# First x tile in halves by two queues, GpSimd in program order, one ScalarE copy ahead of two activations, the z sums in two parts

## The chip, the cores and the metric

One core of one Trainium2 chip. The metric is the device time of one execution in microseconds (us). The spans in the profiles are about 2 us shorter than the times of the same runs. The granted TensorE clock was 0.998 to 1.0. A ratio of two kernels is the mean time of one kernel's fast runs over that of the other's of the same rounds, so it is not quite the ratio of the medians that are quoted.

TensorE is PE, VectorE DVE, ScalarE ACT, GpSimd POOL, SyncE SP; "SPq" and "ACTq" are DMA issues. Tiles whose names begin with ps lie in PSUM, where TensorE writes its results; "to evacuate" is to copy them out. xr is a tile of x that is read back, hn a normalised h1, pk and pqa are phi of k and of q, wgu the gate and up weights.

## The reference, cut to what matters

A transformer block, forward and all gradients (`jax.vjp`), for S = 2048 rows of D = 640 in bf16, that is 16 tiles of 128 rows:

```
q, k, v = split(layernorm(x) @ wqkv)             # 32 heads of 20
phi(t)  = where(t > 0, t + 1, exp(t)) + 1e-6
pq, pk  = phi(q), phi(k)
kv      = einsum("bhsd,bhse->bhde", pk, v);  z = pk.sum over s
o       = (pq @ kv) / (pq . z + 1e-6)
h       = x + o @ wo
out     = h + (silu(layernorm(h) @ w_gate) * (layernorm(h) @ w_up)) @ w_down
# returned: out and the gradients of x and of the weights
```

## The kernel before

The first place is the k/q loop (0 to 58 us): per tile, VectorE takes the row statistics, GpSimd makes the reciprocal root, VectorE normalises, TensorE transposes, ScalarE copies the transpose out of PSUM, TensorE multiplies by the k and q weights, ScalarE makes exp and relu, VectorE joins them to pk and pqa.

```python
load_x(nc.sync, 0, 1)                       # x tile 0
load_x(nc.scalar, 1, 2)                     # x tile 1
nc.sync.dma_start(out=wqk[:, 0:3, D:2 * D], in_=w_k[:, 0:3, :])    # k weights, 480 KB
nc.sync.dma_start(out=wqk[:, 3:5, D:2 * D], in_=w_k[:, 3:5, :])    # 320 KB
# ... x tile 2, q weights, ... issued once the statistics of tile 0 are done

def ln_rstd(mv, rstd, t0, nt, eng=nc.gpsimd):
    v = small.tile([P, 4], FP32, name="lnv", tag="lnv")
    eng.tensor_scalar(out=v[:, :nt], in0=mv[:, :nt, 1], scalar1=1e-5, scalar2=None, op0=ALU.add)
    nc.gpsimd.tensor_tensor(out=rstd[:, t0:t0 + nt], in0=v[:, :nt], in1=nhalf[:, :nt], op=ALU.pow)

with tc.manual_schedule(engines={EngineType.PE, EngineType.DVE, EngineType.Activation}):
    # ... cut: tile 0, warm-up matmuls, statistics of tiles 1 and 2
    kq_mm(1, 0)()                           # k of tile 1, then its exp and relu
    kq_mm(0, 1)()                           # q of tile 0, then its exp and relu
    for t in range(1, ST):
        if t == 1:
            ln1(2)                          # normalise, transpose, copy tile 2
        if t > 1:
            kq_mm(t, 0, (lambda: ln1(t + 1)) if t + 1 < ST else None)()
        # ... cut: kq_phi (VectorE), statistics of tile t + 2
        kq_mm(t, 1)()
    ps = mm("ps_z")                         # sums of pk over all rows
    for ci, (n0, n1) in enumerate(NCH):     # two column halves
        for t in range(ST):
            nc.tensor.matmul(ps[q:q + H, ci, :320], lhsT=ones[:, :H], rhs=pk[:, t, n0:n1], ...)
```

The order of the engines named in `manual_schedule` is that of the program; GpSimd isn't among them, so the scheduler places its instructions. After z comes ps_y; its first matmul is the milestone that I use for "end of the first stage".

The second place is the stage from about 108 to 149 us, in which x is read back for the residual, tile by tile, while the first group of gate and up weights is loaded:

```python
def load_xr(t):
    if t < ST:
        xrs[t] = wk("xr")                   # one of 5 work buffers
        nc.sync.dma_start(out=xrs[t][:], in_=x_v[:, t, :])

for t in range(ST + 2):
    if t < ST:
        # ... cut: ps_a = attention output of tile t
        nc.vector.tensor_tensor(out=half(xr[:]), in0=row(ps), in1=half(xr[:]), op=ALU.add)   # h1
        # ... cut: its statistics
        dm(1)                               # ps_dm matmuls, ScalarE evacuates them to dmst
    if t > 0:
        load_xr(t + 2)
    # ... cut
    nc.scalar.dma_start(out=scr_h1_v[:, u, :], in_=h1[:])            # store of h1, u = t - 2
    # ... cut: hn, and its transpose by DMA

def load_wgu(g):
    nc.sync.dma_start(out=t[:, :, 0:w], in_=B_w_gate[...])           # 560 KB
    nc.sync.dma_start(out=t[:, :, w:2 * w], in_=B_w_up[...])         # 560 KB
```

Of the kernel before, what the change touches and what calls it, by code (L numbers as in the profile page):

```python
# [13 lines left out]
EngineType = mybir.EngineType  # L14
# [6 lines left out]
def kernel(  # L21
# [8 lines left out]
    nc = tc.nc  # L30
# [3 lines left out]
    ST = S // P  # L34
    DT = D // P
    NCH = [(0, 320), (320, 640)]
# [12 lines left out]
    x_v = A_x.rearrange("b (t p) d -> p (b t) d", p=P)  # L49
# [13 lines left out]
    def mm(name):  # L63

        return psum.tile([P, 2, 512], FP32, name=name, tag="mm")

    def row(ps):
        return ps[:, :, :320]

    def half(ap):  # L70
        return ap.rearrange("p (c n) -> p c n", c=2)
# [3 lines left out]
    def wk(name, w=D, pool=0):  # L75
        return wpools[pool].tile([P, w], BF16, name=name, tag="w", padded_shape=[P, D])
# [99 lines left out]
    def fw(name):  # L176
        return wpool.tile([P, 2, GM], BF16, name=name, tag="f", bufs=6)
# [9 lines left out]
    x_tm = [strips.tile([P, 8, D], BF16, name="x_tm", tag="S") for _ in range(2)]  # L187
# [6 lines left out]
    def load_x(eng, t0, t1):  # L194
        return eng.dma_start(out=x_tm[t0 // 8][:, t0 % 8:(t1 - 1) % 8 + 1, :], in_=x_v[:, t0:t1, :])

    load_x(nc.sync, 0, 1)
    load_x(nc.scalar, 1, 2)
    w_k = A_wqkv[:, D:2 * D].rearrange("(k p) n -> p k n", p=P)
    w_q = A_wqkv[:, 0:D].rearrange("(k p) n -> p k n", p=P)  # L200
# [3 lines left out]
    def wait_for(on, dmas):  # L204
        info = mybir.DependencyInfo(mybir.DependencyClass.Sync, mybir.DependencyReason.DATA)
        for dma in dmas:
            tc.add_manual_dep(dma.ins, on.ins.name, info, reason="paced")
# [7 lines left out]
    def load_3():  # L215
        for t0 in range(4, ST, 2):
            yield load_x(nc.sync, t0, t0 + 2)
        yield nc.sync.dma_start(out=wvo[:, 0:5], in_=A_wqkv[:, 2 * D:3 * D].rearrange("(k p) n -> p k n", p=P))
        for j in range(HG):
            yield nc.sync.dma_start(out=wvo[:, 5 + j, :], in_=A_wo[OH[j]:OH[j] + P, :])  # L220
        yield load_wdT(wdT, 0)
        for c in range(4):
            yield nc.sync.dma_start_transpose(out=dh2T[:, :, c * 512:(c + 1) * 512], in_=go_flat[c * 512:(c + 1) * 512, :])
        yield load_wdT(wdT, 1)
        yield load_wdT(wdT3, 3)
# [38 lines left out]
    def ln1_stats(t):  # L264
        st = ln_stats(x_tm[t // 8][:, t % 8, :], mv1[:, t, :])
        if t == 0:
            wait_for(st, load_2())

    def ln1_xn(t):
        nc.vector.tensor_scalar(out=xn[:, t, :], in0=x_tm[t // 8][:, t % 8, :], scalar1=mv1[:, t, 0:1],  # L270
                                scalar2=rstd1[:, t:t + 1], op0=ALU.subtract, op1=ALU.mult)

    def ln1_rstd(t):
        ln_rstd(mv1[:, t:t + 1, :], rstd1, t, 1)

    def ln1(t):
        if t < NC:
            nc.vector.tensor_scalar(out=xn[:, t, :], in0=x_tm[t // 8][:, t % 8, :], scalar1=mv1[:, t, 0:1],
                                    scalar2=None, op0=ALU.subtract)
        else:  # L280
            ln1_xn(t)
        tp = psum.tile([P, D], BF16, name="ps_t", tag="mm")
        for kt in range(DT):
            nc.tensor.transpose(tp[:, kt * P:(kt + 1) * P], xn[:, t, kt * P:(kt + 1) * P], ident[:])
        tpv = tp[:].rearrange("p (k c) -> p k c", c=P)
        if t == 0:
            wait_for(nc.scalar.copy(out=xnT[:, t, 0:3], in_=tpv[:, 0:3]), load_3())
            nc.scalar.copy(out=xnT[:, t, 3:5], in_=tpv[:, 3:5])
        else:
            nc.scalar.copy(out=xnT[:, t], in_=tpv)  # L290

    def kq_mm(t, which, between=None):
        dst, w0 = ((pk, D), (pqa, 0))[which]
        ps = mm("ps_kq")
        for k0, k1 in ((0, 3), (3, DT)) if t == 0 else ((0, DT),):
            for ci, (n0, n1) in enumerate(NCH):
                for k in range(k0, k1):
                    nc.tensor.matmul(ps[:, ci, :320], lhsT=xnT[:, t, k, :], rhs=wqk[:, k, w0 + n0:w0 + n1],  # L298
                                     start=(k == 0), stop=(k == DT - 1))
            if between and (t > 0 or k0 == 0):  # L300
                between()

        def act():
            e = fw("phi_e")
            r = fw("phi_r")
            sc = rstd1[:, t:t + 1] if t < NC else 1.0
            nc.scalar.activation(out=e[:, :, :320], in_=row(ps), func=ACT.Exp, scale=sc)
            nc.scalar.activation(out=r[:, :, :320], in_=row(ps), func=ACT.Relu, scale=sc)  # L308
            ers.setdefault(t, []).append((dst, e, r))

        return act

    def kq_phi(t, last=True):
        n = len(ers[t]) if last else 1
        for _ in range(n):
            dst, e, r = ers[t].pop(0)
            nc.vector.tensor_scalar(out=e[:, :, :320], in0=e[:, :, :320], scalar1=1.0, scalar2=1e-6,
                                    op0=ALU.min, op1=ALU.add)
            nc.vector.tensor_tensor(out=half(dst[:, t, :]), in0=e[:, :, :320], in1=r[:, :, :320], op=ALU.add)
        if last and t % 4 == 3:  # L320
            sl = slice(t - 3, t + 1)
            nc.sync.dma_start(out=scr_pk_v[:, sl, :], in_=pk[:, sl, :])
            nc.sync.dma_start(out=scr_pq_v[:, sl, :], in_=pqa[:, sl, :])
            nc.sync.dma_start(out=scr_xnT[sl].rearrange("t p k c -> p t k c"), in_=xnT[:, sl])

    with tc.manual_schedule(engines={EngineType.PE, EngineType.DVE, EngineType.Activation}):

        ps = mm("ps_warm")

        def warm(n):  # L330
            for _ in range(n):
                nc.tensor.matmul(ps[:, 0, :P], lhsT=ident[:], rhs=ident[:], start=True, stop=True)

        warm(31)
        ln1_stats(0)
        ln1_rstd(0)
        ln1(0)
        warm(12)
        ln1_stats(1)
        ln1_rstd(1)  # L340
        kq_mm(0, 0, lambda: ln1(1))()
        ln1_stats(2)
        ln1_rstd(2)
        kq_mm(1, 0)()
        kq_mm(0, 1)()
        for t in range(1, ST):
            if t == 1:
                ln1(2)
            if t > 1:
                kq_mm(t, 0, (lambda: ln1(t + 1)) if t + 1 < ST else None)()  # L350
            if t == 2:
                kq_phi(0)
            if t + 2 < ST:
                ln1_stats(t + 2)
                ln1_rstd(t + 2)
            if t == 1:
                kq_phi(0, last=False)
            kq_mm(t, 1)()
            if t > 1:
                kq_phi(t - 1)  # L360
            if t >= ST - NC:
                ln1_xn(t - ST + NC)
        kq_phi(ST - 1)


        ps = mm("ps_z")
        for ci, (n0, n1) in enumerate(NCH):
            for t in range(ST):
                q = t % 4 * H
                nc.tensor.matmul(ps[q:q + H, ci, :320], lhsT=ones[:, :H], rhs=pk[:, t, n0:n1],  # L370
                                 start=(t < 4), stop=(t >= ST - 4))
        zs = [wk("zs"), wk("zl")]
        nc.scalar.copy(out=half(zs[0][:]), in_=row(ps))
        last_zs = nc.vector.tensor_tensor(out=half(zs[1][:]), in0=row(ps), in1=half(zs[0][:]), op=ALU.subtract).ins
        ps_z = mm("ps_zb")
# [599 lines left out]
```

## Time and profile before

| | kernel before |
|---|---|
| time, 3 runs | 822.63 us (822.4 to 823.15) |
| span of the profiled run | 820.8 us |
| TensorE busy | 814.0 us, 99% |
| first statistics / third copy / first ps_y | 3.96 / 13.46 / 57.68 us |

How to read it: TensorE is busy nearly all the time, so only its idle time can be won. The lines that carry this stand in the prediction.

### The profile page before, as it was taken

Reading aid. Unit: us, or ns where it says so; the run is one execution under the profiler, and the core shown is the slowest. Engines: PE = TensorE matmul, PEld = TensorE weight load, DVE = VectorE, ACT = ScalarE, POOL = GpSimd, SP = SyncE. Lnnn points to the kernel's source line nnn. Section 1 sums busy time; section 2 is a strip of 40 time slices with the busy share of each in tenths; the row PEclk is TensorE's granted clock in tenths of the full one; section 3 lists DMA queues with packets and bytes.
Section 4 is the critical chain, followed back from the end, with each engine's and each line's share of the span. In section 5 each row is a group of like instructions: output and inputs, shape, how many; then the busy total and the mean of one; then the engine's idle time right before and its main releaser. Section 6 shows DMA issues by size and latency. Waiting matters only on the chain.

```text
span 820.8 us, 14051 instructions
## 1 busy us (share of the span) xinstructions
PE 814.0 (99%) x5540; PEld 523.4 (64%) x5540; DVE 443.8 (54%) x875; ACT 291.5 (36%) x412; POOL 187.4 (23%) x345
## 2 busy tenths in 40 slices
PE   8999999999999999999999999999999999999998
PEld 6776656555555555555566677777776777777776
DVE  6888686891087018800760157887884366631222
ACT  6982422770184126400841122323312133322101
POOL 2330022322412412221125301211210121112330
PEclk9999999999999999999999999999999999999999
DMA  9994589998769997894498757985497989899952
GB/s 295 194 351 95 141 183 276 306 203 176 191 127 209 199 220 168 185 246 111 107 244 180 246 141 213 217 209 161 124 235 172 165 162 176 170 185 258 257 155 73
DMA packets 278241, 158.53 MB, mean 193 GB/s; under 512 B 235036, under 2 KB 264797, under 8 KB 278176
## 3 DMA queue, kind: packets, MB, share of 16 engines
q1 hardware_dynamic: 251616, 82.04, 52.7%
q0 software_dynamic: 17744, 64.45, 24.9%
q10 hardware_dynamic: 8816, 11.16, 4.3%
q8 instruction: 43, 0.70, 0.3%
q14 instruction: 22, 0.18, 0.1%
HBM read 47.60 MB, written 53.66 MB: 123 GB/s over the span
## 4 chain that ended last, share of the span: by engine, by line
PE 87%; DVE 6%; ACT 3%; DMA 2%; issue 1%; SPq 1%; POOL 0%; DVEq 0%; ACTq 0%
PE ps_dw L627 21%; PE ps_dhn L109 14%; PE ps_dxn L877 8%; PE ps_o L932 7%; PE pu L563 7%; PE pg L558 7%; PE ps_dwqk L109 5%; PE ps_y L109 3%; PE ps_dp L109 3%; PE ps_dk L109 3%; PE ps_gt L678 3%; PE pdm L385 2%; PE ps_dm L385 2%; DVE st L134 1%; ACT phi_r L308 1%; DMA xr<-in_A_x_dram 1%
## 5 line engine op out<-in xcount | busy, mean ns | idle before, releaser
L109 PE MATMUL ps_dhn<-wgT,cols 128*128 128x320 bf16 x864 | 119.5, 299 | 0.0
L627 PE MATMUL ps_dw<-dd,hn 128*128 128x448 bf16 (+1 forms) x640 | 118.8, 346 | 0.0
L109 PEld LDWEIGHTS <-cols 128*128 128x128 bf16 x864 | 84.5, 98 | 32.9
L627 PEld LDWEIGHTS <-hn 128*128 128x128 bf16 x640 | 62.6, 98 | 54.2
L629 DVE CAST dwev<-ps_dw 128x896 bf16<-128x896 f32 (+3 forms) x12 | 10.9, 907 | 123.2 <-PE ps_dw L627 123.2
L629 ACT CAST dwev<-ps_dw 128x896 bf16<-128x896 f32 (+1 forms) x20 | 17.6, 878 | 157.9 <-PE ps_dw L627 157.9
L592 POOL DMA_DIRECT2D scr_dT<-stg x64 | 34.6, 541 | 168.9 <-DMA stg<-dd 168.0
L147 DVE CUSTOM_DVE_ANT_0 lb_a<-lb_dy,hn 128x640 bf16<-128x640 bf16 x32 | 26.4, 825 | 75.4 <-ACT lb_dy L145 75.4
L563 PE MATMUL pu<-wgu,hnT 128*128 128x448 bf16 (+1 forms) x320 | 63.6, 346 | 0.0
L558 PE MATMUL pg<-wgu,hnT 128*128 128x448 bf16 (+1 forms) x320 | 63.6, 346 | 0.0
L932 PE MATMUL ps_o<-wd,mT 128*128 128x320 bf16 (+2 forms) x462 | 62.8, 295 | 0.0
L627 PE MATMUL ps_dw<-m_s,dh 128*128 128x448 bf16 (+1 forms) x320 | 60.4, 346 | 0.0
L877 PEld LDWEIGHTS <-ring 128*128 128x128 bf16 x480 | 47.0, 98 | 18.2
L932 PEld LDWEIGHTS <-mT 128*128 128x128 bf16 x462 | 44.0, 98 | 16.2 <-issue 0.3
L877 PE MATMUL ps_dxn<-wqkvT,ring 128*128 128x320 bf16 x320 | 51.3, 299 | 0.0
L627 PEld LDWEIGHTS <-dh 128*128 128x128 bf16 x320 | 31.3, 98 | 27.1
L563 PEld LDWEIGHTS <-hnT 128*128 128x128 bf16 x320 | 31.3, 98 | 27.1
L558 PEld LDWEIGHTS <-hnT 128*128 128x128 bf16 x320 | 31.3, 98 | 27.0
L385 PEld LDWEIGHTS <-dh2T 128*128 128x128 bf16 x320 | 31.1, 98 | 25.5 <-issue 0.6
L298 PE MATMUL ps_kq<-wqk,xnT 128*128 128x320 bf16 x320 | 46.4, 299 | 1.0 <-ACT xnT L290 1.0
L385 PE MATMUL ps_dm<-wdT,dh2T 128*128 128x448 bf16 (+1 forms) x240 | 46.9, 344 | 0.3 <-ACT dmst L399 0.2
L145 ACT ACTIVATE lb_dy<-ps_dhn,rstd 128x640 bf16<-128x640 f32 x16 | 12.7, 793 | 87.8 <-PE ps_dhn L109 87.8
(163 smaller groups left out, 1277.5 us busy)
## 6 DMA issues: line engine op xcount, KB each, us to landing
scr_dT<-stg POOLq DMA_DIRECT2D x48, 224.0 KB, 3.2
cols<-scr_dT POOLq DMA_DIRECT2D x6, 1728.0 KB, 8.5
scr_m<-m_s POOLq DMA_DIRECT2D x12, 448.0 KB, 4.5
cols<-scr_dT ACTq DMA_DIRECT2D x2, 1728.0 KB, 9.7
out_dram<-dwev POOLq DMA_DIRECT2D x30, 112.0 KB, 3.0
scr_dT<-stg POOLq DMA_DIRECT2D x16, 192.0 KB, 2.6
scr_pk<-pk SPq DMA_DIRECT2D x4, 640.0 KB, 7.8
scr_pq<-pqa SPq DMA_DIRECT2D x4, 640.0 KB, 8.1
```

The lines of the kernel that those rows point to most:

```text
L109: nc.tensor.matmul(ps[:, ci, :320], lhsT=lhs(k), rhs=rhs(k, *NCH[ci]), start=(start and k == 0), stop=(stop and k == n - 1))
L147: nc.vector.tensor_tensor_reduce(out=a[:], in0=dy[:], in1=xhat, scale=1.0, scalar=0.0, op0=ALU.mult, op1=ALU.add, accum_out=sums[:, 1:2])
L298: nc.tensor.matmul(ps[:, ci, :320], lhsT=xnT[:, t, k, :], rhs=wqk[:, k, w0 + n0:w0 + n1], start=(k == 0), stop=(k == DT - 1))
L385: nc.tensor.matmul(ps[:, c, :w], lhsT=dh2T[:, kt, (t + c) * P:(t + c + 1) * P], rhs=wdT[:, kt, o:o + w], start=(kt == 0), stop=(kt == DT - 1))
L558: nc.tensor.matmul(pg[:, c, :w], lhsT=hnT[:, kt, (t + c) * P:(t + c + 1) * P], rhs=wg[:, kt, 0:w], start=(kt == 0), stop=(kt == DT - 1))
L563: nc.tensor.matmul(pu[:, c, :w], lhsT=hnT[:, kt, (t + c) * P:(t + c + 1) * P], rhs=wg[:, kt, w:2 * w], start=(kt == 0), stop=(kt == DT - 1))
L592: nc.gpsimd.dma_start(out=scr_dT[t + c, :, KO[g]:KO[g] + GK[g], :], in_=stg[:, :GK[g], :])
L627: nc.tensor.matmul(ps[:, c, :w], lhsT=lhs(t), rhs=rhs(t), start=(t == 0), stop=(t == ST - 1))
L629: copy(out=ev[:, :len(parts), :w], in_=ps[:, :len(parts), :w])
L678: nc.tensor.matmul(ps[:, ci, :320], lhsT=dh1[:, t, i * P:(i + 1) * P], rhs=pqs_tm[:, t, n0:n1], start=(t == 0), stop=(t == ST - 1))
L877: nc.tensor.matmul(ps[:, ci, :320], lhsT=lhs[:, i, :], rhs=rhs[:, i, n0:n1], start=(k == 0 and i == 0), stop=(k == 2 and i == DT - 1))
L932: nc.tensor.matmul(po, lhsT=mT[:, t % 4, j, :], rhs=wd[:, j, n0:n1], start=(j == 0), stop=(j == FT - 1))
```

## The change

Its intent: begin sooner (the first tile in halves by two queues, the second behind it), give the first root sooner (GpSimd in program order), and close TensorE's hole at 14 us (the third transpose is copied before the exp and relu of q of tile 0). It also does the z sums in two parts, tiles 0 to 11 first, which its description doesn't mention.

```diff
-    load_x(nc.sync, 0, 1)
+    nc.sync.dma_start(out=x_tm[0][:, 0, 0:320], in_=x_v[:, 0, 0:320])
+    nc.scalar.dma_start(out=x_tm[0][:, 0, 320:640], in_=x_v[:, 0, 320:640])
     load_x(nc.scalar, 1, 2)
@@
-    with tc.manual_schedule(engines={EngineType.PE, EngineType.DVE, EngineType.Activation}):
+    with tc.manual_schedule(engines={EngineType.PE, EngineType.DVE, EngineType.Activation, EngineType.Pool}):
@@
-        kq_mm(0, 1)()
+        act = kq_mm(0, 1)
+        ln1(2)
+        act()
         for t in range(1, ST):
-            if t == 1:
-                ln1(2)
@@
-        for ci, (n0, n1) in enumerate(NCH):
-            for t in range(ST):
+        for ci, (n0, n1), t0, t1 in [(c, NCH[c], *r) for r in ((0, 12), (12, ST)) for c in range(2)]:
+            for t in range(t0, t1):
```

## The prediction

> **What bounds the kernel now.** I read the page's busy line first, then TensorE's waits, then the timeline of the first 20 us and of 55 to 58 us, because the diff touches nothing later.
>
> ```profile
> PE 814.0 (99%) x5540; PEld 523.4 (64%) x5540; DVE 443.8 (54%) x875; ACT 291.5 (36%) x412; POOL 187.4 (23%) x345
> ```
>
> TensorE is busy for 814.0 of 820.8 us, and the change removes no matmul. All it can win is idle time: 6.8 us, part of it the unavoidable beginning and end. The view of TensorE's waits (us in total, times, longest) says where that idle time is:
>
> ```profile
> PE ps_warm L332 <- POOL ident masks.py:199: 1.4, 1, 1.4
> PE ps_kq L298 <- ACT xnT L290: 1.0, 2, 0.8
> PE ps_t L284 <- DVE xn L278: 0.7, 1, 0.7
> PE ps_dm L385 <- ACT dmst L399: 0.2, 1, 0.2
> ...
> PE ps_z L370 <- DVE pk L319: 0.2, 1, 0.2
> ```
>
> The change aims at the second, third and last of these, 1.9 us or 0.23% of the time. So the answer is "within 2%" before any detail, and the work is to find the tenths. The timeline of the start (start, duration, what, idle before it):
>
> ```profile
> 0.79 0.40 ACTq L195 DMA_DIRECT2D x_tm<-in_A_x_dram  x1
> ...
> 0.80 0.40 SPq L195 DMA_DIRECT2D x_tm<-in_A_x_dram  x1
> ...
> 3.96 0.89 DVE L134 BATCH_NORM_STATS2 st<-x_tm 128x6 f32<-128x320 bf16 x2 [2.59 <-DMA x_tm<-in_A_x_dram]
> ...
> 8.78 1.62 POOL L140 TENSOR_TENSOR rstd<-lnv,nhalf 128x1 f32<-128x1 f32 x3
> ...
> 9.39 0.79 ACT L307 ACTIVATE phi_e<-ps_kq,rstd 128x640 bf16<-128x640 f32 x1 [0.50 <-POOL rstd L140]
> ...
> 10.44 0.45 DVE L270 TENSOR_SCALAR xn<-x_tm,mv,rstd 128x640 bf16<-128x640 bf16 x1 [1.90 <-POOL rstd L140]
> ...
> 13.46 0.73 ACT L290 COPY xnT<-ps_t 128x640 bf16<-128x640 bf16 x1
> ...
> 14.25 1.53 PE L298 MATMUL ps_kq<-wqk,xnT 128*128 128x320 bf16 x10 [0.77 <-ACT xnT L290]
> ```
>
> Three things are to be seen. Nothing starts before the first x tile lands (3.96 us). GpSimd makes the first reciprocal root only at 8.78 us, after the "lnv" of all three first tiles, which holds ScalarE for 0.50 and VectorE for 1.90 us. ScalarE copies the third transpose at 13.46 us, behind six phi passes, though it was ready at about 12.1 us; TensorE stands for it.
>
> **What the Trainium skill says.** "DMA: Bandwidth & Descriptors", section "Issuing engines are not separate DMA queues": transfers from any engine run on the same 16 DMA engines and interleave; a second issuer saves only issue time. The trace agrees: the two 160 KB x tiles, issued together, took 3.14 and 3.0 us to land, the third, issued at 5.12 us nearly alone, 2.26 us. Its section "Queues, rings and completion order" adds that each DMA engine goes round its queues by packets. So the halves win nothing by using two queues as such; they win because the second tile no longer shares the engines with the first. "SBUF — State Buffer", section "SBUF: two separate sides": VectorE and GpSimd hold a shared port pair exclusively. The trace fits: the root takes 0.54 us (1.62 / 3) while VectorE is idle, 0.82 us beside its work later.
>
> **The change, part by part.** Against before, only three engine streams move: the first load is split, with ScalarE issuing one more DMA; GpSimd's order becomes lnv, root, lnv, root, lnv, root; and ScalarE's third copy moves ahead of phi(q) of tile 0. The order of VectorE is the same, and TensorE's differs only in the z sums.
>
> *Split load.* The first bytes move at 1.8 us; by 2.8 us 194 KB have moved, by 3.2 us 338 KB. The tile alone is 160 KB; with the other one 320 KB. If the two halves are served first, their bytes are in some 0.4 us earlier; rows of 640 instead of 1,280 bytes may take part of that back. Estimate: 0.35 us, range 0 to 0.6. The chain from there (statistics 0.89, aggregate 0.21, xn 0.39, transposes, copy 0.48, first k matmuls) is bound link by link until the matmuls at 8.95 us, so TensorE gets it in full, and the paced loads behind it move with it. The weights don't hold it: the DMA engines were empty from about 5.5 to 6.0 us. The second x tile lands later, but VectorE takes it only at 5.43 us, 1.6 us after it landed.
>
> *GpSimd's order.* The first root moves from 9.3 us to before 6.5, so phi of tile 0 starts 0.6 us earlier (about 8.8, after the copy). The third root comes at about 9.4 instead of 10.4, so xn of tile 2 is 1 us earlier. TensorE gains nothing by itself: it is in the matmuls from 8.95 to 11.7 us.
>
> *Third copy first.* Its transposes end at 11.68 + 0.44 = 12.12 us, so the copy runs 12.14 to 12.83 instead of 13.46 to 14.19. The ten matmuls of 11.96 us issue every 0.136 us until 13.32, so the next ten start there instead of 14.25. The hole is worth 0.93 us.
>
> *What the loop takes back.* phi(q) of tile 0 moves from 12.11 to 12.74, its second pass from 12.79 to 13.41, ending at 14.2. VectorE, in fixed order, waits for it: pqa of tile 0 starts at about 14.25 instead of 13.96, and VectorE has no slack after that (9.2 of 10 us busy). So pk of tile 1 ends at 16.5 instead of 16.2. The phi buffers hold three pairs, so ScalarE's first phi of tile 2 must wait for it: 16.6, where it could have been 16.0. That delays the PSUM slot for the transposes of tile 4 (17.98 instead of 17.67), the copy behind it, and the matmuls of tile 4: 19.73, where a closed hole would give 19.4 and before had 20.25. I worked the four engines forward in this way through all 16 tiles with the trace's spacings (matmul 0.136, transposes 0.27, phi 0.593, copy 0.60, VectorE 3.01 per tile). The same working gives before's z stage an end at 57.56 us, where the trace has 57.68, so I trust it to 0.1 us. About 0.42 us of 0.93 is left at the end of the loop.
>
> *z in two parts.* The lines:
>
> ```profile
> 56.01 0.72 PE L370 MATMUL ps_z<-pk,ones 128*32 128x320 bf16 x15
> 56.91 0.84 PE L370 MATMUL ps_z<-pk,ones 128*32 128x320 bf16 x17 [0.17 <-DVE pk L319]
> 57.68 4.52 PE L109 MATMUL ps_y<-pk,xn 128*128 128x320 bf16 x32
> ```
>
> Half of the z sums need the last pk after 15 matmuls, and the other 17 come behind it. In the new order 27 of 32 need no tile after 14. TensorE arrives 0.42 us earlier, while the last pk is earlier by only 0.26 us; 27 matmuls at 0.043 us cover that wait, and 5 follow instead of 17. The end of z moves from 57.56 to 56.80 in my working: 0.76 us with the 0.42 of the loop. With ScalarE spacings 0.02 us longer it is 0.5. I take 0.65.
>
> Sum: 0.35 + 0.65 = 1.0 us, 822.63 - 1.0 = 821.6 us.
>
> **Rivals.** *The hole closes and stays closed:* 0.93 for the hole, 0.3 for z and 0.35 for the load give 1.6 us, 821.0. For it: TensorE sets the period of the loop (2.997 us a tile), no wait shows after 14.25 us. Against: ScalarE and VectorE run at 3.0 us a tile too, so nothing can lead the others for long. *The loop takes everything back,* the copies return to 19.09, 22.09 and so on, and only load and z remain: about 822.1. For it: in my working ScalarE's fourth copy is at 18.98, no gain at all; it regains 0.3 afterwards because its spacings have 0.03 us of slack. *The split does nothing,* since the fixed latency dominates or the short rows cost what the order wins: 822.0. *A later stage swallows the gain:* the only later wait of TensorE in the first 140 us is 0.2 us at 137 us, on an evacuation whose chain runs through reloads of x (5.59 us for one). That chain starts at a matmul at 87.97 us, so it should move along. If it doesn't: 822.5.
>
> **Range and chances.** The parts are uncertain by about 0.3 us each, and another build's DMA timing and run-to-run spread (822.4 to 823.15) add 0.4. 8 times in 10: 820.8 to 822.5. Faster or slower by 2% would be 16 us; nothing here is that large. Faster 0.005, within 2% 0.99, slower 0.005.
>
> **What would show it.** The first statistics start at about 3.6 us (split right), or at 3.9 (wrong). GpSimd alternates lnv and root, and the first phi starts 0.5 us sooner relative to the first statistics. The 0.77 wait on xnT disappears, but a wait of 0.1 to 0.4 us on xnT, xn or a phi appears by tile 4. The first ps_y matmul comes near 56.7 instead of 57.68 us. All later stages shift by the same amount; if ps_y is early and the end is not, a DMA wait between 90 and 140 us took it. My prediction is wrong if the loop closes fully, or if the first tile lands later than now.

## More of the kernel before

The batches ran on different chips, where the median of the kernel before was 822.59 to 823.5 us, so the order of two variants of different batches that lie a few tenths apart is not shown.

One more of VectorE's timeline is needed later; the columns are start, duration, instruction, operands:

```profile
13.96 0.49 DVE L319 TENSOR_TENSOR pqa<-phi_e,phi_r 128x640 bf16<-128x640 bf16 x1
14.37 0.88 DVE L134 BATCH_NORM_STATS2 st<-x_tm 128x6 f32<-128x320 bf16 x2
```

This is the first pqa, without a wait, and VectorE goes on at once: from here on it runs the loop at 3.015 us a tile. Its one large gap, 0.52 us at 25 us, is in all traces (0.51 to 0.53).

## The result, and the profile after

823.02 us median of 4 runs (822.04 to 823.76), the kernel before 822.59 with one more run beside it. The ratio is 1.0003, 95% interval 0.9986 to 1.0021: no difference, and 1.4 us above the prediction.

TensorE's waits in the profile after (us in total, times, longest):

```profile
PE ps_dm L386 <- ACT dmst L400: 0.8, 1, 0.8
PE ps_dxn L878 <- DMA ring<-dq: 0.5, 1, 0.5
PE ps_t L285 <- DVE xn L271: 0.3, 1, 0.3
PE ps_kq L299 <- ACT xnT L291: 0.2, 1, 0.2
...
PE ps_z L371 <- DVE pk L320: 0.2, 1, 0.2
```

The waits that the change aims at went from 1.9 us to 0.7. (The 0.3 for xn is a new one: it stands in the loop, at 26.5 us.) But the wait for dmst grew from 0.2 to 0.8, and one for a transposed dq came. The start in the timeline (line numbers are one up from before):

```profile
3.02 0.89 DVE L134 BATCH_NORM_STATS2 st<-x_tm 128x6 f32<-128x320 bf16 x2 [1.65 <-DMA x_tm<-in_A_x_dram]
...
5.39 0.89 DVE L134 BATCH_NORM_STATS2 st<-x_tm 128x6 f32<-128x320 bf16 x2 [0.82 <-DMA x_tm<-in_A_x_dram]
...
9.42 0.45 DVE L271 TENSOR_SCALAR xn<-x_tm,mv,rstd 128x640 bf16<-128x640 bf16 x1 [1.00 <-POOL rstd L140]
...
13.55 0.49 DVE L320 TENSOR_TENSOR pqa<-phi_e,phi_r 128x640 bf16<-128x640 bf16 x1 [0.36 <-ACT phi_r L309]
```

The first tile is there 0.94 us earlier, not 0.35. The second, which VectorE took without a wait at 5.43, now makes it wait 0.82 us, so a part of that is lost again: the copy of the second transpose starts at 7.49 us, before at 8.20. The third xn comes at 9.42 as predicted. The copy is where it should be and the hole is closed:

```profile
8.10 0.79 ACT L308 ACTIVATE phi_e<-ps_kq,rstd 128x640 bf16<-128x640 f32 x1
...
11.44 0.69 ACT L291 COPY xnT<-ps_t 128x640 bf16<-128x640 bf16 x1
```

And the end of the stage:

```profile
55.11 1.13 PE L371 MATMUL ps_z<-pk,ones 128*32 128x320 bf16 x27
56.41 0.43 PE L371 MATMUL ps_z<-pk,ones 128*32 128x320 bf16 x5 [0.17 <-DVE pk L320]
56.77 4.52 PE L109 MATMUL ps_y<-pk,xn 128*128 128x320 bf16 x32
```

ps_y starts at 56.77 us; before it was 57.68, and 56.7 was predicted. So 0.91 us were won here. The lead is 0.94 us when the reload of x is issued at 111.86 us (before: 112.80). At 137 us it is nearly gone. Before, then after, in TensorE's timeline:

```profile
137.03 1.79 PE L385 MATMUL ps_dm<-wdT,dh2T 128*128 128x384 bf16 x10 [0.23 <-ACT dmst L399]
```

```profile
136.87 1.79 PE L386 MATMUL ps_dm<-wdT,dh2T 128*128 128x384 bf16 x10 [0.78 <-ACT dmst L400]
```

The same matmul begins only 0.16 us earlier: TensorE came 0.71 us earlier (136.87 - 0.78 against 137.03 - 0.23) and stood for the evacuation. At 710 us comes another wait of 0.46 us for the dq transpose. The span is 0.4 us longer than before; 0.91 won, 0.55 and 0.46 lost account for 0.1 of it, the other 0.3 is not located.

### The profile page after: what moved, and what is told of

The parts are those of the page before. It is cut to its first block, busy times and chain, and to the rows that moved or that the text cites. A ratio compares the mean times of both kernels' runs of the same rounds, so it can differ in the third digit from the quotient of the medians.

```text
span 821.2 us, 14053 instructions
## 1 busy us (share of the span) xinstructions
PE 814.6 (99%) x5540; PEld 522.0 (64%) x5540; DVE 443.9 (54%) x875; ACT 291.6 (36%) x412; POOL 187.8 (23%) x345
## 4 chain that ended last, share of the span: by engine, by line
PE 91%; DVE 4%; ACT 2%; DMA 2%; issue 1%; SPq 0%; POOL 0%; DVEq 0%; ACTq 0%; POOLq 0%
PE ps_dw L628 21%; PE ps_dhn L109 14%; PE ps_o L933 7%; PE ps_dxn L878 7%; PE pu L564 7%; PE pg L559 7%; PE ps_dwqk L109 5%; PE ps_dm L386 5%; PE ps_y L109 3%; PE ps_gt L679 3%; PE ps_dp L109 3%; PE ps_dk L109 2%; PE ps_a L109 2%; PE pdm L386 2%; DVE st L134 1%; DMA ring<-dq 1%
```

## The experiments

Eighteen runs follow, three of them of the two kernels unaltered, each batch on one chip beside the kernel before; each goes by the name that its section gives. "before" and "after" are the first traces of the two kernels. In the tables "x2" and "x3" are the starts of the statistics of the second and third tile, "copy 2" and "copy 3" ScalarE's copies of the second and third transpose, "pqa" VectorE's first pqa.

### The two kernels again (after_again, before_again)

> The changed kernel unaltered, for the spread between traces and a closer mean. Theory A (the gain is made in the first 58 us and taken back by the transfers between 112 and 137 us): ps_y starts near 56.8 us as in the first trace, the wait of ps_dm near 137 us is 0.6 to 0.9 us, the mean time is within 0.4 us of before, and the 0.5 us wait on ring near 710 us need not come again. Theory B (the change itself delays something late in the kernel): the ring wait near 710 us comes again at the same place. Theory C (the first times were only noise): mean 0.7 to 1.0 us below before.

> The kernel before unaltered, a second trace of it. Theory A: ps_y at 57.7 us within 0.05, the wait of ps_dm near 137 us between 0 and 0.5 us because the landing of the x reload near 133.5 us varies by some tenths from run to run. Theory B: no wait on ring. Time ratio 1.000.

Measured: the changed kernel 822.13 us (821.74 to 823.94, 6 runs), ratio 0.9987 (0.9975 to 0.9999); ps_y at 56.85, no wait listed at 137 us and none at 710 us, span 819.9. The kernel before 823.03 (822.68 to 824.41, 5 runs), 57.58, a wait of 0.20 at 137 us, span 821.0. The runs of the kernel before in the same batch: 823.04 (822.49 to 825.16, 11 runs). So the gain of the first stage repeats, the two later waits don't in the list, and one execution differs from the next by more than the gain. The matmuls' starts show more than the list of waits, since the ends of matmuls are modelled. In this second trace of the changed kernel:

```profile
134.58 1.52 PE L109 MATMUL ps_a<-wvo,pqsT 128*128 128x320 bf16 x10
136.25 1.79 PE L386 MATMUL ps_dm<-wdT,dh2T 128*128 128x384 bf16 x10
```

The ps_dm of the tile before starts 1.36 us behind its ps_a (131.60, 132.96), this one 1.67: TensorE was held for 0.31 us here too. Counted in this way the hold is 0.94 us in the first trace of the changed kernel, and 0.40 and 0.37 in the two of the kernel before.

### Parts of the change alone (split_only, no_split, z_only, order_only, after_nocopy, after_halves)

`split_only` has only the first hunk of the diff, `no_split` all but the first.

> Before with the split of the first load alone. The first statistics start near 3.0 us instead of 3.96 and the second x tile lands about 1 us later than before, so TensorE's matmuls of 8.95 us start near 8.25 (0.7 us). Everything to the z sums shifts with it: ps_y near 57.0 us, 0.7 us early, and the 0.77 us hole stays. Theory A: the whole time within 0.4 us of before all the same. Theory C: 0.7 us faster.

> The changed kernel with the first load in one piece as before: GpSimd's order, the early third copy and the z sums alone. My prediction's working gave 0.65 us at ps_y; the changed trace suggests only 0.2 (0.91 in all less 0.71 of the split), since VectorE's stall near 24.5 us is there in both kernels and VectorE sets the pace after it. So ps_y near 57.5 us (0.2) rather than 57.0 (0.65). Theory A: the time equals before within 0.3 us.

Measured: `split_only` 823.62 us (822.16 to 825.12, 6 runs), ratio 1.0 (0.9986 to 1.0014), and ps_y at 58.42, 0.7 us *later* than before: a miss. Its trace:

```profile
6.10 0.89 DVE L134 BATCH_NORM_STATS2 st<-x_tm 128x6 f32<-128x320 bf16 x2 [1.49 <-DMA x_tm<-in_A_x_dram]
```

The second tile made VectorE wait 1.49 us, so the third came late too (8.15 us), and in the old GpSimd order everything hangs on the third. `no_split`: 822.57 us (822.02 to 823.23, 5 runs), ratio 0.9989 (0.9977 to 1.0001), ps_y at 57.13; the hole is closed (copy 3 at 11.83) and yet

```profile
13.93 0.49 DVE L319 TENSOR_TENSOR pqa<-phi_e,phi_r 128x640 bf16<-128x640 bf16 x1 [0.36 <-ACT phi_r L308]
```

the first pqa is where it was before. Both have waits at 137 us, 0.81 and 0.64.

Next, the z sums in two parts alone, on the kernel before (the last hunk):

> The kernel before with the sums of z in two parts alone. The prediction's working has the two-part order let TensorE start on z without the last four tiles' pk. Expected: all before 53 us as in the kernel before, no wait before ps_z but up to 0.2 us before the last five, ps_y at 57.3 to 57.5 instead of 57.6 and 57.7, so 0.2 us; time 822.8. If ps_y is at 57.1 or earlier, the whole gain of the variant without the split (57.13) is that of z, and the order of GpSimd and of the third copy gave nothing.

Measured: 822.77 us (822.29 to 823.91, 5 runs), ratio 0.9995 (0.9982 to 1.0007); ps_y at 57.18, no wait inside z. Counted from copy 3 the start of ps_y is 43.80 us away, and 44.22, 44.21 and 44.22 in three traces with the old z order: 0.42 us, all of it z, twice what I expected. Its ps_y is 0.05 us from that of `no_split` (57.13): beside z, GpSimd's order with the copy first added next to nothing in these two traces.

The order of GpSimd and the copy, without split and z:

> The kernel before with GpSimd in program order and the third copy ahead of phi(q), without the split of the first tile and without the two-part z. Theory V: the hole is gone and the third copy is at 11.8, but the first pqa stays at 13.9 (before: 13.96 and 13.86), the loop stays where it was and ps_y is at 57.5 (before: 57.58 to 57.70), so the hole of 0.87 us is worth 0.1. Theory H: ps_y at 57.1 or earlier. Time: 822.9 under V, 822.5 under H.

Measured: 822.47 us (822.34 to 823.12, 5 runs), ratio 0.9992 (0.998 to 1.0004). The hole is gone (copy 3 at 11.42), but ps_y is at 57.14, a miss against both 57.5 and 57.1: in this trace the tiles landed early (copy 2 at 7.45, where the other traces without the split have 7.71 to 8.28). The pqa at 13.52 is 6.07 us behind copy 2, as in the changed kernel (6.06 and 6.17), so it is the early copy 2 that moved. TensorE, no longer held by its hole, waits for VectorE:

```profile
56.37 0.84 PE L370 MATMUL ps_z<-pk,ones 128*32 128x320 bf16 x17 [0.58 <-DVE pk L319]
```

Now the changed kernel with only the third copy put back behind q's exp and relu of tile 0. In the compiled program one ScalarE instruction changes its place, nothing else:

```diff
-        act = kq_mm(0, 1)
-        ln1(2)
-        act()
+        kq_mm(0, 1)()
         for t in range(1, ST):
+            if t == 1:
+                ln1(2)
```

> The changed kernel with the third transpose's copy put back behind phi(q) of tile 0, so that it differs from the changed kernel in the place of one ScalarE instruction. Theory V (VectorE paces the k/q loop from its first pqa on, at 3.015 us a tile, so a closed TensorE hole is worth only as much as VectorE's start moves; the copy ahead of phi(q) holds that start back by 0.6 us): the TensorE hole comes back, over 1 us, the third copy at 12.6 to 13.0 instead of 11.44 and 11.52, the first pqa at 13.0 instead of 13.55 and 13.63, and ps_y no later than in the changed kernel, 56.4 to 56.8 against 56.77 and 56.85. Theory H (the prediction's: the hole is worth 0.4 to 0.9 us to the start of ps_y): ps_y at 57.2 to 57.7. Time: 822.1 under V, 822.8 under H.

Measured: 821.41 us (821.12 to 822.0, 6 runs), ratio 0.9978 (0.9966 to 0.999), the fastest kernel. Its trace:

```profile
12.84 0.71 ACT L291 COPY xnT<-ps_t 128x640 bf16<-128x640 bf16 x1
...
13.60 1.53 PE L299 MATMUL ps_kq<-wqk,xnT 128*128 128x320 bf16 x10 [0.59 <-ACT xnT L291]
...
13.00 0.49 DVE L320 TENSOR_TENSOR pqa<-phi_e,phi_r 128x640 bf16<-128x640 bf16 x1 [0.36 <-ACT phi_r L309]
...
56.62 4.52 PE L109 MATMUL ps_y<-pk,xn 128*128 128x320 bf16 x32
```

The hole is back (0.59 us, not the 1 us that I expected), the pqa is 0.55 us earlier than in the changed kernel's first trace, and ps_y is no later: VectorE's theory holds in this, and the hole was not worth what it looked like. But only half of VectorE's gain arrives. Counted from copy 2, the pqa comes 0.80 us earlier than in the changed kernel's first trace (5.26 against 6.06) and ps_y 0.40 (48.88 against 49.28), for now TensorE's path from copy 3 sets the end again: 43.78 us, as in `z_only` (43.80).

These traces give rigid distances, which settle the first stage:

| schedule | ps_y counted from | us | traces |
|---|---|---|---|
| order and z as before | x3 (start of the third tile's statistics) | 50.27 to 50.28 | 5 |
| new GpSimd order, z in two parts, copy first | copy 2 | 49.26 to 49.42, mean 49.32 | 8 |
| new GpSimd order, z in two parts, copy back | copy 2 | 48.88 to 49.08, mean 48.93 | 5 |

So putting the copy first costs about 0.4 us (49.32 - 48.93), and the end of the stage is now set by copy 2 rather than by x3. (The table counts later variants too, whose first stage is the same.) Copy 2 was at 7.46 to 8.24 us in eleven traces with the split of the first tile alone (mean 7.76) and at 7.45 to 8.28 in eight without (mean 7.90): 0.14 us for the split, and the scatter of one landing is larger. The two groups also differ in GpSimd's order; with the new order alone the means are 7.72 (ten with the split) and 7.68 (three without), so a gain of the split isn't shown.

The second tile in halves too, to keep it from coming late:

```diff
-    load_x(nc.scalar, 1, 2)
+    nc.sync.dma_start(out=x_tm[0][:, 1, 0:320], in_=x_v[:, 1, 0:320])
+    nc.scalar.dma_start(out=x_tm[0][:, 1, 320:640], in_=x_v[:, 1, 320:640])
```

> The changed kernel with the second x tile in halves by the two queues too, so that it isn't behind a half on one queue and beside the 480 KB of weights on the other. If the second tile's late landing is what the split gives away (VectorE waited for it for 0.82, 0.37 and 1.49 us in the three traces with the split, not at all without it): the wait is under 0.3, the statistics of the second tile start at 4.7 instead of 5.14 to 5.39, the first k matmuls at 7.7 instead of 8.24, ps_y at 56.4. If what it loses is the bandwidth that all the first loads share: the first tile's statistics come no later than 3.3 but the second tile waits as before, and ps_y stays at 56.8. Time: 821.8 in the first case, 822.3 in the second, both within the scatter.

Measured: 822.98 us (822.28 to 823.43, 5 runs), ratio 0.9994 (0.9982 to 1.0007). The second tile is there at 4.58 without a wait, but now the k weights and the third tile are late:

```profile
6.66 0.97 PE L300 MATMUL ps_kq<-wqk,xnT 128*128 128x320 bf16 x6 [0.80 <-DMA wqk<-in_A_wqkv_dram]
```

and ps_y is at 57.29. What one transfer wins here, another loses (expected was ps_y at 56.4 or 56.8).

### The stage between 112 and 149 us (after_deep, before_deep, order_z_deep, after_third, nocopy_deep, and three with _upg, two with _lateup)

The first theory: VectorE waits for the reloads of x (four times, 1.7 to 3.7 us), and so the rest. Deeper reloads, on both kernels; every second tile goes to a buffer of the gate/up stage:

```diff
-            xrs[t] = wk("xr")
+            xrs[t] = wk("xr") if t % 2 else wpool.tile([P, D], BF16, name="xr", tag="f", bufs=6, ...)
-        for t in range(3):
+        for t in range(5):
             load_xr(t)
-                load_xr(t + 2)
+                load_xr(t + 4)
```

> The changed kernel, with the x tiles of the residual read back earlier: every second one in a buffer that is free until the gate/up stage, five loaded ahead instead of three and each reload two tiles earlier, so that VectorE's four waits for them between 112 and 137 us (3.7, 2.7, 2.1 and 1.7 us) go. Theory A (the gain of the first 58 us is made in every run and taken back in that stage, by a wait of TensorE for the evacuation of ps_dm at 137 us that was 0.78 us in one trace and absent in another): ps_y starts at 56.8 as in both traces of the changed kernel, no wait of TensorE for the evacuation near 137 us, the first weight-gradient matmul (ps_dw of the first group) at 178.1 to 178.5 in every trace, time 821.9 median, with less spread than the 821.74 to 823.94 of the changed kernel. Theory C (the wait at 137 us is not what takes the time; times scatter by a microsecond for reasons anywhere): the wait goes, but the median stays within 0.3 of 822.4 and the spread is as large.

> The same deeper reload on the kernel before. Theory A: ps_y at 57.6, the wait at 137 us (0.23 and 0.20 in the two traces of the kernel before) gone, first ps_dw at 179.0, time 822.7; the changed kernel with the deeper reload is faster than this by 0.8 to 0.9 us in the traces and in the median. Theory C: no difference that the scatter of the runs lets through, median 823.0.

Measured: 822.06 us (821.59 to 822.88, 5 runs), ratio 0.9982 (0.9968 to 0.9995), and 822.77 (822.33 to 823.5, 5 runs), ratio 0.9992 (0.998 to 1.0005); 0.7 us between the two medians. No wait at 137 us is listed in either (by the starts of the matmuls a hold of 0.24 us is left in the first), and VectorE waits for TensorE (0.68 us a tile) instead of for reloads. Yet ScalarE evacuates no sooner: the store of h1 ahead of it is issued at 135.34 us, though VectorE's part was done, so it isn't the reload that this store waits for. But the two traces didn't obey the rest: ps_y of the first was at 57.30, as the second tile came late again (wait of 1.07 us), and the other one had a new wait of TensorE of 0.9 us at the gate matmuls for a transposed hn, its first ps_dw at 179.90.

Without split, with the third copy back, z in two parts and the deeper reload:

> A candidate to beat both kernels: no split, GpSimd in program order, the third copy left behind phi(q), z in two parts, and the deeper reload of x. Theory V: first pqa at 13.2, ps_y at 56.6 to 56.9 without the split's scatter of the second tile, no wait of TensorE near 137 us, first ps_dw at 178.3, time 822.0 (the changed kernel with the deeper reload had 822.06, the kernel before in the same rounds 823.26). Theory H: the open hole costs 0.4 or more, ps_y at 57.2 or later, time 822.7.

Measured: 821.52 us (821.44 to 821.82, 5 runs), ratio 0.998 (0.9968 to 0.9992); ps_y 56.77, no wait at 137 us, ps_dw 177.91. As fast as the variant above, without the split.

The changed kernel a third time, and the best parts together:

> The changed kernel once more, for a third trace and six more times. Theory S (ps_y comes 0.4 to 0.9 us sooner in every trace, and what is left of it at the end depends on two waits of TensorE that come and go by chance, near 137 us for the evacuation of ps_dm and near 710 us for a transposed dq): ps_y at 56.7 to 57.3, the span equal to ps_y plus these two waits plus 763.0 within 0.3 us, the median between 822.0 and 822.8, and 0.4 to 1.0 us below the kernel before of the same rounds. Theory R (the first result, 823.02 against 822.6, was the rule and the second, 822.13, the chance): median 822.8 to 823.3 and no difference to the kernel before.

> A candidate to beat all: the changed kernel with the third copy back behind phi(q) of tile 0 and with the deeper reload of x. Expected from the two alone (821.41 without the deeper reload, 822.06 with it and the copy ahead): ps_y at 56.5 to 56.9, no wait near 137 us, first ps_dw at 177.8 to 178.2, median 821.2 to 821.6, about 1.7 us below the kernel before of the same rounds. If the wait near 137 us is absent without the deeper reload as well, as it was in the only trace of the variant with the copy back, the deeper reload adds nothing and 821.4 is repeated.

Measured: the changed kernel 823.02 us (822.66 to 823.48, 5 runs), ratio 1.0005 (0.9992 to 1.0019). That is theory R's number, with theory S's cause in the trace: ps_y at 56.97, and

```profile
137.10 1.78 PE L386 MATMUL ps_dm<-wdT,dh2T 128*128 128x384 bf16 x10 [1.01 <-ACT dmst L400]
```

a wait of 1.01 us; the span is 56.97 + 1.01 + 762.8. The other kernel: 821.56 us (821.09 to 823.04, 5 runs), ratio 0.9989 (0.9977 to 1.0002), no wait at 137 us; it doesn't beat 821.41.

What is TensorE waiting for? ScalarE's timeline of the changed kernel's first trace:

```profile
135.65 0.33 ACTq L530 DMA_DIRECT2D scr_h<-xr  x1
136.02 0.80 ACT L400 CAST dmst<-ps_dm 128x768 bf16<-128x768 f32 x1 [4.14 <-DVE hn L531]
```

The evacuation stands behind the issue of a store of h1. The profile names VectorE's hn as the releaser, but that hn ran from 135.41 to 135.80, past the issue at 135.65, so it can't be what the store waited for. The store's own data, VectorE's residual add, was ready at 134.33:

```profile
133.51 0.82 DVE L514 TENSOR_TENSOR xr<-ps_a,xr 128x640 bf16<-128x640 f32 x1 [2.05 <-DMA xr<-in_A_x_dram]
```

"PSUM — Partial Sum Buffer", section "Engine vs sequencer instructions", of the Trainium skill says that ScalarE's queue is strictly first in, first out; the trace agrees, the evacuation follows 0.37 us behind the issue. What the store waits for is in the compiled program, which lists the semaphores of each instruction:

```
(SyncE)    L183 DMACopy wgu<-in_B_w_up_dram 128x5x448 [waits DMAHW1_49]
(ScalarE)  L530 DMACopy scr_h_78<-xr 128x640 [waits DMAHW1_49,DVE_49]
```

The up weights (560 KB) and this store use the same semaphore; I read it as taking turns, the later being issued when the earlier has landed. SyncE issued the weights at 127.93 us:

```profile
DMA to landing us min/median/max: 7.7/7.7/7.7
```

(the answer for the tile wgu in the window of that issue). 127.93 + 7.7 = 135.63, the store is issued at 135.65. The other two traces of the changed kernel: 127.36 + 7.6 = 134.96 and 135.03; 127.9 + 7.9 = 135.8 and 135.88. The kernel before: 128.44 + 7.3 = 135.74 and 135.81. (The sums are of rounded numbers; by the traces' own landing times each store is 0.07 to 0.08 us behind.) So the weights moved to GpSimd's queue:

```diff
-        nc.sync.dma_start(out=t[:, :, w:2 * w], in_=B_w_up[...])
+        (nc.gpsimd if g == 0 else nc.sync).dma_start(out=t[:, :, w:2 * w], in_=B_w_up[...])
```

> The changed kernel with the 560 KB of the first group's up weights issued by GpSimd instead of SyncE. In the compiled program ScalarE's store of an h1 tile (issued at 135.65 us in the first trace) waits for the same semaphore as that load, which SyncE issued at 127.9 us and which landed 7.7 us later; the evacuation of ps_dm is behind the store, TensorE behind the evacuation. Theory W (that landing, not the reloads of x as such, is what TensorE waits for near 137 us, and it doesn't move with ps_y): with the load on another queue and semaphore the store is issued before 135.0 in the trace, no wait of TensorE near 137 us in the trace, first ps_dw at ps_y plus 121.4 to 121.7, median 821.7 to 822.1, spread under 1.5. Theory X (the reloads of x hold the chain): the store is still at 135.4 or later and the wait of 0.6 to 1.0 comes back, median 822.7.

> The same on the kernel before. Theory W: ps_y 57.6, no wait near 137 us, first ps_dw at 179.0 to 179.2, median 822.5 to 822.8: little changes, as the kernel before waits there for only 0.2. The changed kernel with the same edit is then faster than this by what the first stage gives, 0.6 to 0.9 us. Theory X: the wait of 0.2 stays, and the two stay equal within 0.3.

> A candidate to beat all: the changed kernel with the third copy back behind phi(q) of tile 0 and the up weights issued by GpSimd. ps_y 56.5 to 56.9, no wait near 137 us, median 821.2 to 821.6; against the same kernel without the edit of the weights (821.41) no difference if the wait rarely comes there, as its narrow spread (821.12 to 822.0) suggests.

Measured: 824.97 us (824.45 to 827.1, 6 runs), ratio 1.0029 (1.0016 to 1.0042); 824.74 (823.46 to 827.78, 6 runs), ratio 1.0024 (1.0008 to 1.004); 823.85 (823.11 to 825.47, 5 runs), ratio 1.0013 (1.0001 to 1.0025). All three are slower, by 0.1 to 0.3%: a clear miss for theory W as I had put it. GpSimd issued the weights 3 us earlier, at 124.9, in front of reloads that were still to come:

```profile
137.16 1.52 PE L109 MATMUL ps_a<-wvo,pqsT 128*128 128x320 bf16 x10 [2.35 <-DVE xr L514]
```

TensorE waits 2.35 us for the residual add (0.64 and 0.77 in the other two). The add waited for its reload of x, which took 8.81 us to land (127.35 to 136.16) against 6.08 in the changed kernel's first trace. So the weights and the reloads compete. The same traces also settle what held the store. It follows its add at once, 0.03 us behind its end at 137.11:

```profile
136.28 0.82 DVE L514 TENSOR_TENSOR xr<-ps_a,xr 128x640 bf16<-128x640 f32 x1 [5.27 <-DMA xr<-in_A_x_dram]
```

```profile
137.14 0.33 ACTq L530 DMA_DIRECT2D scr_h<-xr  x1
```

So do, by 0.03 us, the two stores during the weights' flight (127.36 and 129.57 us; the weights landed at 131.06). In the packed traces this store and the weights name one semaphore for their landing in 15 of the 20 traces; in all 15 the store is issued 0.07 to 0.08 us behind that landing and 1.32 to 3.96 us behind its add. In the other five, the three with _upg and the two with _lateup, they share none, and it is issued 0.03 us behind its add. So the shared semaphore holds the store, and the competition of the transfers is a second effect, which this edit made worse. Then the weights should go later, behind the reload of x tile 12:

```diff
+        up = ExitStack()
+        if g == 0:
+            up.enter_context(tc.issue_after(xr_dma[12].ins))
+        with up:
             nc.sync.dma_start(out=t[:, :, w:2 * w], in_=B_w_up[...])
```

> The changed kernel with the up weights of the first group issued by SyncE as before, but behind the reload of x tile 12, some 5 to 8 us later (133 to 136 us; they are needed at 149.4). ScalarE's store no longer shares their semaphore in the compiled program, and the reloads have the DMA engines to themselves for longer. Theory W in its second form (the 560 KB of up weights among the reloads set the end of the stage, by the shared semaphore and by the shared DMA engines; moving them earlier made it worse by 2.35 us): no wait of TensorE near 137 us, none of over 0.3 up to 149 us, first ps_dw at ps_y plus 121.4 to 121.7, that is 178.3 to 178.8, median 821.7 to 822.2. If the reloads alone hold the stage: a wait of 0.6 to 1.0 near 137 us again, median 822.7. If the weights come too late now: a wait before the gate or up matmuls at 149 us, and 823 or more.

> A candidate to beat all: the same on the changed kernel with the third copy back behind phi(q) of tile 0. ps_y 56.5 to 56.9, no wait near 137 us, median 821.2 to 821.6; if the late weights cost something at 149 us, above 822.

Measured: 822.67 us (821.87 to 823.4, 4 runs), ratio 0.9991 (0.9976 to 1.0005), the kernel before 823.5 (12 runs, 11 of them those of the batch before on the same chip); and 822.17 (821.36 to 822.96, 4 runs), ratio 0.9987 (0.9973 to 1.0002). The weights are issued at 137.7 us in the first, and

```profile
134.33 0.33 ACTq L535 DMA_DIRECT2D scr_h<-xr  x1
134.70 0.80 ACT L404 CAST dmst<-ps_dm 128x768 bf16<-128x768 f32 x1 [3.57 <-DVE xr L519]
```

the store goes out 1.3 us earlier than in the changed kernel's first trace; no wait at 137 us, first ps_dw at 178.53, 121.3 behind ps_y. In the trace the second theory holds for this stage. In the times it was missed: 821.7 to 822.2 and 821.2 to 821.6 were expected. Both kernels have a small new wait at 181 us (0.48 and 0.16), and neither beats 821.41. The changed kernel's 15 runs have a median of 822.7, so that this wait is what keeps its time up is not shown.

### The account

The span of each trace is the start of ps_y, plus TensorE's waits after 62 us (leaving out the 0.2 us near 620 us that all have), plus a constant:

| trace | ps_y | later waits | span | rest |
|---|---|---|---|---|
| before | 57.68 | 0.23 | 820.8 | 762.9 |
| before_again | 57.58 | 0.20 | 821.0 | 763.2 |
| before_deep | 57.70 | 0.9 | 821.7 | 763.1 |
| split_only | 58.42 | 0.81 | 822.1 | 762.9 |
| after | 56.77 | 0.78 + 0.46 | 821.2 | 763.2 |
| after_again | 56.85 | none | 819.9 | 763.1 |
| after_third | 56.97 | 1.01 | 820.8 | 762.8 |
| after_nocopy | 56.62 | none | 819.3 | 762.7 |
| after_upg | 56.90 | 2.35 | 822.2 | 763.0 |
| after_lateup | 57.20 | 0.48 + 0.20 | 821.3 | 763.4 |

The ten other traces lie between 762.8 and 763.5. So the larger differences of the spans come from two things: when ps_y starts, and which of the later waits it meets. The rest still scatters by 0.8 us, as much as the first stage won, and that isn't explained.

## Why the prediction was wrong, by its own steps

*Split, 0.35 us.* Direction right, size wrong. The first tile won 0.94, 0.74 and 0.90 us (against 3.96; the eight traces without the split have 3.51 to 3.96, mean 3.80), but "the second x tile lands later, but VectorE takes it only at 5.43 us, 1.6 us after it landed" failed: behind the half and beside 800 KB of k weights it landed so late that VectorE waited 0.37 to 1.49 us in the eleven traces with this split alone. On average 0.14 us remain, or nothing where GpSimd's order is the same. That all issuers share the same DMA engines stands in the prediction, and the traces agree; I applied it to the first tile and not to the second.

*GpSimd's order.* Right: the third xn at 9.42 against a predicted 9.4.

*Third copy first, and what the loop takes back (0.42 of 0.93 left).* Closing the hole is right (copy 3 at 11.44 to 11.83), the remainder isn't. The prediction saw that the copy delays the first pqa, but it charged only the phi buffers for it, and the wait that it expected by tile 4 comes only at 26.5 us. The two limits of the loop, TensorE from copy 3 (44.21 us) and VectorE from the pqa (43.62 us: 57.14 - 13.52), gave 57.67 and 57.58 us in the kernel before, 0.1 apart; so the hole was worth 0.1. The copy in front takes about 0.4 us from what GpSimd's order gives. This is the rival "the loop takes everything back".

*z.* Undersized: with the loop's 0.42 it had 0.65 in all, which leaves 0.23; alone it was 0.42.

*Their sum, 1.0 us.* Measured from the mean of the two traces of the kernel before (57.63): 0.86, 0.78 and 0.66 us in the three traces of the changed kernel. The sum is a quarter too large, with errors in the terms that partly cancel. That doesn't explain the 1.4 us.

*The step that failed* is the one that dismissed the later stage: "That chain starts at a matmul at 87.97 us, so it should move along." It moves along only roughly. TensorE's arrival at the matmul of 137 us does move with ps_y (79.1 to 79.3 us behind it). But the evacuation is behind a store that waits for the landing of the up weights, and in the ten traces that hold TensorE there the matmul starts 1.29 to 1.31 us behind that landing. The landing was 78.06 and 78.11 us behind ps_y in the two traces of the kernel before, and 78.80, 78.10 and 78.84 in the three of the changed kernel. So the matmul starts at 137.03 and 136.99 before, at 136.87, 136.25 and 137.10 after, though ps_y is 0.66 to 0.86 us earlier; in `split_only`, with ps_y at 58.42, it starts at 138.45, so it isn't a fixed time either. The chain doesn't hang on the reloads of x in the way that the prediction took it to: with the reloads early (`after_deep`, add done at 131.38) the store still went out at 135.34, behind the landing. The prediction gave this rival 822.5, and its own list of signs named the case: "if ps_y is early and the end is not, a DMA wait between 90 and 140 us took it."

*The range.* The 0.4 us for another build and the run-to-run spread rested on three runs. The 61 runs of the kernel before lie between 821.8 and 825.46 (median 823.03), the 15 of the changed kernel between 821.74 and 823.94 (median 822.7). The starting value of 822.63 was itself a little low, and a range of 1.7 us was too narrow for a median of four. In the second batch the changed kernel's median, 822.13, was inside it; which batch one gets is luck.

What stays open: how much of the 1.4 us in the timed runs is the hold at 137 us, for one trace each can't tell, and the variants without it differ in time (822.67 and 822.17 with the late weights, 821.41 to 821.56 for three others with the copy put back); why the hold was only 0.31 us in the changed kernel's second trace (the landing was 0.6 to 0.9 us earlier there, nothing shows why); and whether the wait is rarer with the copy put back, which the narrow spread of that kernel's six runs suggests but one trace can't show. The dq wait at 710 us (0.3 to 0.7 us, in 4 of the 20 traces, three of them of kernels other than the changed one, and 0.2 in a fifth) wasn't tested.

## What to carry to other kernels

When two engines pace a loop to within a tenth of a microsecond, a hole on one of them is worth only the distance to the other: look for the first instruction after which the other engine never idles, and ask whether the edit delays *that*. An early gain reaches the end only if each later wait moves with it. Where the releaser that a profile names doesn't fit the times, look for a landing that shares a semaphore. Here 560 KB moved ahead of the small reloads brought a wait of 0.64 to 2.35 us, and moved behind them ended the wait at 137 us in the trace, though not visibly in the time. Where two starts that belong together move apart, TensorE was held, even if no wait is listed. Before predicting tenths, take the spread from many more than three runs.

## What the Trainium skill lacked or had wrong

- No page tells that a semaphore which transfers of different engines share can hold one of them back for another. "DMA: Bandwidth & Descriptors" warns of two transfers in flight on one semaphore ("Why a DMA increments its semaphore by 16 and not by 1"), but because of stale data, not of delay. Its section "Two DMAs through the same engine are not ordered", which names the completion semaphore as the means of order, is where the delay belongs. In 15 traces a store of 160 KB was issued 0.07 to 0.08 us behind the landing of 560 KB of weights, 1.32 to 3.96 us after its own data was ready; in the five traces in which they share no semaphore it was 0.03 us.
- The same page, section "Issuing engines are not separate DMA queues", says that a second issuer saves only the time to initiate. For the first tile the two halves saved 0.74 to 0.94 us of landing, and the second tile paid with 0.37 to 1.49 us of wait. The page is not contradicted, as the same engines move both, but it doesn't say that the choice of queue can decide which transfer is late: with the second tile in halves too (`after_halves`) it came without a wait, and TensorE waited 0.80 us for the k weights.
